# Seven half-size products instead of eight for the second feed-forward layer, in a DeltaNet kernel with a pipelined feed-forward

## The chip, the cores and the metric

The kernel runs on one core of a Trainium2 chip. The metric is the device time of one execution in microseconds (us). Each kernel is run several times beside the kernel before on the same chip; quoted are medians with the lowest and highest run. The granted clock is the share of PE's full clock rate that a trace shows as granted. Engines are named as in the profile: PE (TensorE matmuls), PEld (its weight loads), DVE (VectorE), ACT (ScalarE), POOL (GpSimd).

## The reference

Everything is fp32: a DeltaNet attention, whose state depends on every earlier token, then a feed-forward network with exact gelu.

```python
# batch, n_heads, seq, head_dim = 4, 8, 768, 48;  d_model, d_ff = 384, 2048
for t in range(S):
    kt, vt, bt = k_n[:, :, t], v[:, :, t], beta[:, :, t, None]
    y[:, :, t] = einsum('bhd,bhde->bhe', q[:, :, t], state)
    v_old = einsum('bhde,bhd->bhe', state, kt)
    state = state + bt[..., None] * einsum('bhd,bhe->bhde', kt, vt - v_old)
x = y as (3072 tokens, 384)
h = x @ w_in                          # (3072, 2048)
g = 0.5 * h * (1 + erf(h / sqrt(2)))
out = g @ w_out                       # (3072, 384)
```

## The kernel before

The sequence is cut into 12 chunks of 64 tokens. A chunk has two units (`a` = 0, 1) of 128 rows: two batches of 64 tokens each. The attention of a later chunk runs beside the feed-forward of an earlier one; a plan gives each step a time, steps are emitted in that order, DVE keeps this order exactly, and a scheduler orders PE. In this document **window w** is the stretch from the first matmul of the hidden layer (psH) of chunk w-1 to that of chunk w. Every second window, the odd ones from 3 to 9, holds an elimination: DVE inverts 32x32 triangles of two chunks row by row. Even windows hold the join, in which PE makes larger inverses from these (psJ, two levels).

```python
def products(u, part=(0, 1)):          # K K^T and K Q^T in one product of 128 columns
    ...
    nc.tensor.matmul(psG[HALF[p], r, j, cols], lhsT=u.KQt[rows, p, j, 0, :],
                     rhs=u.KQt[rows, p, j].rearrange("q x n -> q (x n)")[:, cols], ...)
    ...                                # P, the masked K Q^T: one DVE product per unit

def eliminate(j):                      # 30 rows, a chain on DVE
    nc.vector.tensor_tensor(tmp, ..., op=ALU.mult)
    nc.vector.tensor_tensor(nu[:, j + 1:, 0:j], nu[:, j + 1:, 0:j], tmp, op=ALU.add)

def back(x):                           # three transposes on DVE: XM, then Zf twice
    ...
def join(g, ts, level):                # psJ on PE: needs XM, then Zf
    ...

def fc1(c, f):                         # hidden layer, f = 0..15
    for m in range(NM):
        nc.tensor.matmul(psH, lhsT=w_in_sb[:, m, f*128:(f+1)*128], rhs=xTs[c][:, m, :], ...)
    nc.scalar.activation(gs[f], psH, ACT.Gelu)

def fc2(u, f0, f1):                    # second layer: 16 products of 384 columns per unit
    for f in range(f0, f1):
        nc.tensor.matmul(u.psO, lhsT=gs[f][:, u.a*128:(u.a+1)*128], rhs=w_out_sb[:, f, :], ...)
    if f1 == NF:
        nc.scalar.copy(o_sb, u.psO)    # then two stores
```

Of the kernel before, what the change touches and what calls it, by code (L numbers as in the profile page):

```python
# [16 lines left out]
def kernel(  # L17
# [47 lines left out]
    start = ExitStack()  # L65
    su = start.enter_context(tc.tile_pool(name="su", bufs=2))
# [4 lines left out]
    def sq(name, *shape):  # L71
        return ps.tile([128, *shape], F32, tag="sq", name=name)


    NKS, NQS, NKW = 6, 4, 10
    Kp = [cpool.tile([128, H, C], F32, name=f"Kp{i}") for i in range(NKS)]


    KQb = [cpool.tile([128, 2, NP, 2, 2, HB], F32, name=f"KQb{i}") for i in range(NQS // 2)]
    Qp = [b.rearrange("q p j x h n -> q (p j x h n)").rearrange("q (o h n) -> q o h n", o=2, h=H)[:, o]  # L80
          for b in KQb for o in range(2)]
# [9 lines left out]
    K_late = []  # L91
# [7 lines left out]
    for c in range(NC):  # L99
        for a in range(NA):  # L100
            u = tiles[c, a] = Unit()
            u.c, u.a, u.n = c, a, c * NA + a
            u.t = (c % 2) * NA + a
            u.Qp = Qp[u.n % NQS]
            u.KQb = KQb[a]
            if u.n < NKW:
                u.Kp = Kp[u.n % NKS]

    def load(c):
        if c >= NC:  # L110
            return
        for a in range(NA):
            u = tiles[c, a]
            if u.n >= NKW:
                u.Kp = K_late[(u.n - NKW) % len(K_late)]
            fetch_in(u.Kp[:, :, 0:D], k, u)
            if c < 4:
                fetch_in(u.Qp[:, :, 0:D], q, u)

    def load_blocks(c):  # L120
        for a in range(NA):
            u = tiles[c, a]
            for x, src in enumerate((k, q)):
                src = src.rearrange("b h t d -> (b h) t d")[2 * a * H:2 * (a + 1) * H]
                for h in range(2):
                    rows = slice(c * C + h * HB, c * C + (h + 1) * HB)
                    for r in range(2):
                        for e in range(2):
                            w = min(HB, D - e * HB)
                            to = slice((2 * r + e) * HB, (2 * r + e + 1) * HB)  # L130
                            nc.sync.dma_start(
                                out=u.KQb[to, :, :, x, h, 0:w].rearrange("q p j n -> q (p j) n"),
                                in_=src[r::2, rows, e * HB:e * HB + w].rearrange("n t d -> t n d"))
# [38 lines left out]
    Zf = [cpool.tile([128, NU, C], F32, name=f"Zf{i}") for i in range(2)]  # L172
    St = cpool.tile([128, NA, 2, NP, D], F32)
# [82 lines left out]
    def squares(u, n, engine=None):  # L256
        kd = u.Kp[:, :, 0:D]
        ksq = wk.tile([128, H, D], F32, tag="ksq", name="ksq")
        if engine is None:
            nc.scalar.activation(ksq, kd, ACT.Square)  # L260
        else:
            engine.tensor_tensor(ksq, kd, kd, op=ALU.mult)
        nc.vector.tensor_reduce(n, ksq, axis=AX.X, op=ALU.add)
# [33 lines left out]
    def transposed(u, part=(0, 1)):  # L297
        if 0 in part:
            u.KQt = wk.tile([128, 2, NP, 2, C], F32, tag="KQt", name="KQt", bufs=6)
        for x in part:  # L300
            psT = sq("psT", NP, 128)
            flat = (u.Kp, u.Qp)[x].rearrange("q h d -> q (h d)")
            for j in range(NP):
                nc.tensor.transpose(psT[:, j, :], flat[:, j * 128:(j + 1) * 128], ident)
            nc.scalar.copy(u.KQt[:, :, :, x, :].rearrange("q p j n -> q j p n"),  # L305
                           psT.rearrange("q j (p n) -> q j p n", p=2))

    def turned(u):
        u.KQt = wk.tile([128, 2, NP, 2, C], F32, tag="KQt", name="KQt", bufs=6)
        nc.vector.transpose(u.KQt.rearrange("q p j x n -> q (p j x n)"),  # L310
                            u.KQb.rearrange("q p j x h n -> q (p j x h n)"))

    def products(u, part=(0, 1)):
        g = u.c // 2
        cols = slice(part[0] * C, (part[-1] + 1) * C)
        psG = dn("psG").rearrange("q r (j n) -> q r j n", j=NP)
        for j in range(NP):
            for r, p in QUADS:
                rows = slice(r * C, r * C + D)
                nc.tensor.matmul(psG[HALF[p], r, j, cols], lhsT=u.KQt[rows, p, j, 0, :],  # L320
                                 rhs=u.KQt[rows, p, j].rearrange("q x n -> q (x n)")[:, cols],
                                 start=True, stop=True)
        if 0 in part:
            if u.t == 0:
                Gs[g] = wk.tile([128, NU, HB], F32, tag="G", name="G", bufs=1)
            span = slice(u.t * H, (u.t + 1) * H)
            nc.scalar.copy(heads(Gs[g][:, span]), psG[:, :, :, HB:C])
            if g > 0:
                if u.t == 0:
                    Ds[g] = wk.tile([128, NU, HB], F32, tag="diag", name="diag", bufs=1)  # L330
                nc.scalar.copy(heads(Ds[g][:, span]), psG[:, :, :, 0:HB])  # L331
                for p in range(2):
                    lower = slice(p * C + HB, (p + 1) * C)
                    nc.scalar.copy(Ds[g][lower, span], Gs[g][lower, span])
        if 1 in part:
            u.P = wk.tile([128, H, C], F32, tag="P", name="P", bufs=6)
            if u.c < 2:
                nc.scalar.copy(heads(u.P), psG[:, :, :, C:])
            else:
                nc.vector.tensor_tensor(heads(u.P), psG[:, :, :, C:], heads(mask_h), op=ALU.mult)  # L340

    def grams(us):
        for u in us:
            products(u)
# [4 lines left out]
    def diagonals(u):  # L349
# [4 lines left out]
        for j in range(NP):  # L354
            for b in range(2):
                for r, p in QUADS:
                    rows = slice(r * C, r * C + D)
                    blk = u.KQt[rows, p, j, 0, b * HB:(b + 1) * HB]
# [84 lines left out]
    def gram_steps(c):  # L443
        us = [tiles[c, a] for a in range(NA)]
        return ([(1.0, transposed, u) for u in us] if c < 4 else []) + [(2.0, grams, us)]
# [17 lines left out]
    def against_state(us):  # L463

        for u in us:
# [8 lines left out]
            for x in range(2):  # L474
                for j in range(NP):
                    for r, p in QUADS:
                        rows = slice(r * C, r * C + D)
                        to = HALF[p ^ (j % 2)] if x else HALF[p]
                        nc.tensor.matmul(u.psK[to, x, r, j, :], lhsT=u.KQt[rows, p, j, x, :],  # L479
# [90 lines left out]
    gs = {}  # L570

    def fc1(c, f):
# [4 lines left out]
        gs[f] = wk.tile([128, NA * 128], F32, tag=f"g{f}", name=f"g{f}", bufs=1)  # L577
        nc.scalar.activation(gs[f], psH, ACT.Gelu)  # L578

    def fc2(u, f0, f1):  # L580
        if f0 == 0:
            u.psO = ps.tile([128, DM], F32, tag="mlp", name="psO")
        for f in range(f0, f1):
            nc.tensor.matmul(u.psO, lhsT=gs[f][:, u.a * 128:(u.a + 1) * 128],  # L584
                             rhs=w_out_sb[:, f, :], start=(f == 0), stop=(f == NF - 1))
        if f1 == NF:
            o_sb = wk.tile([128, DM], F32, tag="o_sb", name="o_sb")
            nc.scalar.copy(o_sb, u.psO)  # L588
            for p in range(2):
                row = (2 * u.a + p) * S + u.c * C  # L590
                nc.scalar.dma_start(out=out[row:row + C, :], in_=o_sb[HALF[p]])

    def ffn_steps(c):
        steps = [(1.3, fc1, c, f) for f in range(NF)]
# [3 lines left out]
        return steps + twos  # L598
# [47 lines left out]
    for u in first:  # L646
        products(u, (0,))
    for u in first:
        transposed(u, (1,))
        products(u, (1,))  # L650
# [38 lines left out]

    def late():  # L690
        start.close()
        more = ctx.enter_context(tc.tile_pool(name="late", bufs=1))
        for i in range(4):
            K_late.append(more.tile([128, H, C], F32, name=f"Kl{i}"))
            nc.gpsimd.memset(K_late[i][:, :, D:], 0.0)
        K_late.extend(Kp)
# [6 lines left out]
    plan += [at(0.99, 1.0, [(1.0, prep, 2)]), at(1.055, 1.06, [(1.0, finish, 2)]), at(1.6, 1.61, [(1.0, finish, 3)]), at(2.75, 2.76, [(1.0, finish, 4)]), at(1.06, 1.14, gram_steps(2)),  # L703
# [3 lines left out]
             at(2.6, 2.61, [(1.0, prep, 4)]), at(2.8, 2.9, gram_steps(4))]  # L707
    plan += [at(1.62, 1.63, [(1.0, load, 4)]), at(0.995, 1.0, [(1.0, load_v, 2)])]
    plan += [at(c - 0.4, c - 0.3, v_steps(c)) for c in range(2, NC)]
    plan += [at(c - 1.0, c - 0.99, [(1.0, load_v, c)]) for c in range(3, NC)]  # L710
    plan += [at(c - 2.4, c - 2.39, [(1.0, load, c)]) for c in range(5, NC)]
    for c in range(4, NC):
        when = {4: 2.73, 5: 3.03}.get(c, c - (1.6 if c % 2 == 0 else 2.03))
        after = {4: 1.8, 5: 2.76}.get(c, c - (2.94 if c % 2 == 0 else 2.54))
        plan += [at(after, after + 0.01, [(1.0, load_blocks, c)])]
        plan += [at(when, when + 0.02, [(1.0, turned, tiles[c, a]) for a in range(NA)])]
    for w in range(3, NC):
        plan += [at(w + 0.25, w + 0.95, state_steps(w))]
        if w + 2 >= NC:
            continue  # L720
        if w % 2:
            plan += [at(w - 0.16, w - 0.15, [(1.0, prep, w + 2)]), at(w, w + 0.01, [(1.0, finish, w + 2)]),
                     at(w + 0.06, w + 0.2, gram_steps(w + 2)),
                     at(w + 0.2, w + 0.95, eliminate_steps(w // 2 + 1)),
                     at(w + 1.02, w + 1.2, join_steps(w // 2 + 1))]
        else:
            plan += [at(w + 0.35, w + 0.36, [(1.0, prep, w + 2)]), at(w + 0.5, w + 0.51, [(1.0, finish, w + 2)]),
                     at(w + 0.45, w + 0.9, gram_steps(w + 2))]
# [32 lines left out]
```

## Time and profile before

| | before |
|---|---|
| median | 717.74 us (717.25 to 717.81, 3 runs) |
| profiled span | 717.4 us |
| PE, DVE busy | 93%, 55% |
| odd windows 3, 5, 7, 9 | 50.0 us each |
| even windows 4, 6, 8, 10 | 54.9, 54.8, 54.8, 52.7 us |
| windows 11, 12 | 46.8, 45.8 us |

The busy shares and slices, and the windows, are shown in the prediction below. Beside them the page gives the chain of work that ended last, followed back from the end of the program, first by engine and then by line:

```profile
PE 74%; DVE 3%; ACT 2%; issue 0%
PE psO L584 32%; PE psH L575 28%; PE psJ L426 3%; PE psK L479 3%; PE psG L320 2%; PE psU L505 2%; PE psY L523 1%; DVE Nu L386 1%; DVE tmp L384 1%; ACT Zf L441 1%; PE psY L532 1%; PE psX L561 1%; DVE XM L395 0%; ACT g L578 0%; DVE Nu L377 0%
```

Nearly the whole chain is PE, and the two feed-forward layers (psO and psH) are 60% of the span. So the second layer looks like the place to save.

### The profile page before, as it was taken

Reading aid. Unit: us, or ns where it says so; the run is one execution under the profiler, and the core shown is the slowest. Engines: PE = TensorE matmul, PEld = TensorE weight load, DVE = VectorE, ACT = ScalarE, POOL = GpSimd, SP = SyncE. Lnnn points to the kernel's source line nnn. Section 1 sums busy time; section 2 is a strip of 40 time slices with the busy share of each in tenths; the row PEclk is TensorE's granted clock in tenths of the full one; section 3 lists DMA queues with packets and bytes.
Section 4 is the critical chain, followed back from the end, with each engine's and each line's share of the span. In section 5 each row is a group of like instructions: output and inputs, shape, how many; then the busy total and the mean of one; then the engine's idle time right before and its main releaser. Section 6 shows DMA issues by size and latency. Waiting matters only on the chain.

```text
span 717.4 us, 19222 instructions
## 1 busy us (share of the span) xinstructions
PE 667.7 (93%) x8404; PEld 496.9 (69%) x8404; DVE 392.5 (55%) x871; ACT 225.3 (31%) x570; POOL 84.7 (12%) x91
## 2 busy tenths in 40 slices
PE   6549797798999999999999999999999999999997
PEld 5447563485678678678678677687687687686774
DVE  6989999999347963337942437933547911211000
ACT  3326453431434124342132333133243133132210
POOL 5051000311301020011020110020211000000000
PEclk9999899997999999999999999999999999999999
DMA  9906735430244201441102441002201000000000
GB/s 139 227 2 145 207 89 155 92 67 1 43 59 63 52 14 26 71 58 28 35 14 32 70 56 24 13 13 40 42 12 24 13 13 2 22 3 12 12 1 22
DMA packets 137252, 36.06 MB, mean 50 GB/s; under 512 B 130064, under 2 KB 133136, under 8 KB 137168
## 3 DMA queue, kind: packets, MB, share of 16 engines
q1 hardware_dynamic: 131120, 29.52, 21.6%
q10 hardware_dynamic: 5952, 5.12, 3.0%
q8 instruction: 66, 1.08, 0.6%
q0 software_dynamic: 96, 0.20, 0.1%
q14 instruction: 18, 0.15, 0.1%
HBM read 30.08 MB, written 4.72 MB: 49 GB/s over the span
## 4 chain that ended last, share of the span: by engine, by line
PE 74%; DVE 3%; ACT 2%; issue 0%
PE psO L584 32%; PE psH L575 28%; PE psJ L426 3%; PE psK L479 3%; PE psG L320 2%; PE psU L505 2%; PE psY L523 1%; DVE Nu L386 1%; DVE tmp L384 1%; ACT Zf L441 1%; PE psY L532 1%; PE psX L561 1%; DVE XM L395 0%; ACT g L578 0%; DVE Nu L377 0%
## 5 line engine op out<-in xcount | busy, mean ns | idle before, releaser
L584 PE MATMUL psO<-w_out_sb,g 128*128 128x384 f32 x768 | 266.0, 496 | 7.5 <-DVE w_out_sb L226 7.3
L575 PE MATMUL psH<-xT,w_in_sb 128*128 128x256 f32 x1152 | 264.5, 386 | 4.1 <-DVE w_in_sb L226 2.5
L575 PEld LDWEIGHTS psH<-xT,w_in_sb 128*128 128x128 f32 x1152 | 216.7, 191 | 41.1 <-ACT g L578 4.5
L584 PEld LDWEIGHTS psO<-w_out_sb,g 128*128 128x128 f32 x768 | 142.6, 192 | 100.7 <-DVE w_out_sb L226 13.9
L578 ACT ACTIVATE g<-psH 128x256 f32<-128x256 f32 x192 | 73.7, 384 | 152.5 <-PE psH L575 151.8
L485 DVE TENSOR_TENSOR W<-psK,V 128x384 f32<-128x384 f32 x22 | 12.2, 553 | 99.6 <-PE psK L479 74.6
L384 DVE TENSOR_TENSOR tmp<-Nu 128x30 f32<-128x30 f32 (+9 forms) x180 | 62.6, 348 | 6.0
L386 DVE TENSOR_TENSOR Nu<-Nu,tmp 128x30 f32<-128x30 f32 (+9 forms) x180 | 61.5, 342 | 6.2
L340 DVE TENSOR_TENSOR P<-psG,mask 128x512 f32<-128x512 f32 x20 | 13.6, 690 | 79.4 <-ACT diag L331 79.3
L274 POOL TENSOR_TENSOR n<-n,half 128x16 f32<-128x16 f32 x10 | 29.5, 2947 | 93.8 <-DMA Zf<-in_moe_w_out_dram 60.6
L546 DVE TENSOR_TENSOR x<-psY,y 64x192 f32<-64x192 f32 x88 | 31.1, 353 | 17.2 <-PE psY L523 16.3
L511 ACT COPY U<-psU 64x192 f32<-64x192 f32 x92 | 28.8, 313 | 33.4 <-PE psU L505 32.1
L294 POOL TENSOR_TENSOR V<-V,n 128x384 f32<-128x384 f32 x20 | 16.8, 844 | 185.6 <-DMA V<-in_v_dram 114.4
L588 ACT COPY o_sb<-psO 128x384 f32<-128x384 f32 x24 | 11.5, 480 | 81.0 <-PE psO L584 79.7
L562 ACT COPY xT<-psX 128x384 f32<-128x384 f32 x24 | 11.3, 478 | 81.2 <-PE psX L561 81.2
L320 PE MATMUL psG<-KQt 48*64 48x128 f32 (+1 forms) x896 | 28.7, 285 | 4.1 <-ACT KQt L305 2.7
L320 PEld LDWEIGHTS psG<-KQt 48*64 48x64 f32 x896 | 24.9, 157 | 10.3 <-issue 4.3
L426 PE MATMUL psJ<-XM,G 32*32 32x32 f32 x768 | 15.6, 203 | 14.9 <-DVE XM L395 14.9
L217 ACT ACTIVATE w_e<-w_e,lim 128x384 uint32<-128x384 uint32 (+2 forms) x31 | 19.3, 625 | 28.8 <-DVE w_e L215 28.7
L408 POOL MEMSET Zf<- 32x512 f32 x23 | 12.2, 529 | 130.1 <-DVE Zf L399 99.1
L426 PEld LDWEIGHTS psJ<-XM,G 32*32 32x32 f32 x768 | 14.8, 119 | 17.3 <-POOL W L469 11.6
L479 PEld LDWEIGHTS psK<-St,KQt 48*64 48x64 f32 x1408 | 22.1, 137 | 6.1 <-issue 4.0
(97 smaller groups left out, 535.5 us busy)
## 6 DMA issues: line engine op xcount, KB each, us to landing
V<-in_v_dram SPq DMA_DIRECT2D x48, 96.0 KB, 3.0
w_out_sb<-in_moe_w_in_dram SPq DMA_DIRECT2D x9, 512.0 KB, 5.5
out_dram<-o_sb ACTq DMA_DIRECT2D x48, 96.0 KB, 2.2
Zf<-in_moe_w_out_dram SPq DMA_DIRECT2D x8, 384.0 KB, 4.2
w_raw<-in_moe_w_out_dram SPq DMA_DIRECT2D x8, 384.0 KB, 3.8
Kp<-in_k_dram SPq DMA_DIRECT2D x28, 96.0 KB, 4.0
KQb<-in_k_dram SPq DMA_DIRECT2D x64, 32.0 KB, 2.2
KQb<-in_q_dram SPq DMA_DIRECT2D x64, 32.0 KB, 2.2
```

The costliest lines, as they stand in the source:

```text
L217: nc.scalar.activation(e, e, ACT.Relu, bias=lim[:, 0:1], scale=float(2 ** 23))
L274: nc.gpsimd.tensor_tensor(flat, flat, half, op=ALU.pow)
L320: nc.tensor.matmul(psG[HALF[p], r, j, cols], lhsT=u.KQt[rows, p, j, 0, :], rhs=u.KQt[rows, p, j].rearrange("q x n -> q (x n)")[:, cols], s ...
L384: nc.vector.tensor_tensor(tmp, nu[:, j + 1:, j:j + 1].to_broadcast([128, n, j]), nu[:, j:j + 1, 0:j].to_broadcast([128, n, j]), op=ALU.mult)
L386: nc.vector.tensor_tensor(nu[:, j + 1:, 0:j], nu[:, j + 1:, 0:j], tmp, op=ALU.add)
L426: nc.tensor.matmul(psJ[to, i // (2 * H), i % (2 * H), :], lhsT=(xm if level else off)[rows, u, :], rhs=zf[rows, u, HB:C] if level else xm[ ...
L479: nc.tensor.matmul(u.psK[to, x, r, j, :], lhsT=u.KQt[rows, p, j, x, :], rhs=St[rows, u.a, p, j, :], start=True, stop=True)
L511: copy(pairs(u.U[HALF[p]], s), u.psU[HALF[p ^ s], p])
L546: nc.vector.tensor_tensor(dst, src, pairs(u.y[HALF[p ^ s]], s), op=ALU.add)
L575: nc.tensor.matmul(psH, lhsT=w_in_sb[:, m, f * 128:(f + 1) * 128], rhs=xTs[c][:, m, :], start=(m == 0), stop=(m == NM - 1))
L578: nc.scalar.activation(gs[f], psH, ACT.Gelu)
L584: nc.tensor.matmul(u.psO, lhsT=gs[f][:, u.a * 128:(u.a + 1) * 128], rhs=w_out_sb[:, f, :], start=(f == 0), stop=(f == NF - 1))
```

## The change

The intent is to save an eighth of the second layer on PE. Unit a of a chunk gives the rows of a 2x2 block matrix, the halves of the 2048 hidden values its columns, `a11 a12 / a21 a22`; w_out is cut likewise into B11, B12, B21, B22. Winograd's form of Strassen's scheme makes the product from seven half products p1 to p7, each of 8 matmuls of 192 columns (two instructions each), with sums before and after:

```diff
+    def sums_of_w():                  # once, on POOL: T1 = B12-B11, T2 = B22-T1, T4 = B21-T2
+        for n, a, b in ((1, B12, B11), (2, B22, 1), (4, B21, 2)):
+            T[n] = more[0].tile([128, FH, DH], F32, name=f"T{n}")
+            nc.gpsimd.tensor_tensor(T[n], a, b if n == 1 else T[b], op=ALU.subtract)
+    def last_sum_of_w():              # T3 = B22-B12
+    ...
+    def mix(c, n, h):                 # DVE, 128x512 each, in two halves
+        if n == 1:                    # S = a21+a22;  a21 <- a11-a21
+            nc.vector.tensor_tensor(W2["S"][:, fs], a21, a22, op=ALU.add)
+            nc.vector.tensor_tensor(a21, a11, a21, op=ALU.subtract)
+        elif n == 2:                  # a11 <- S-a11, once p1 has read a11
+            nc.vector.tensor_tensor(a11, W2["S"][:, fs], a11, op=ALU.subtract)
+        else:                         # a12 <- a12-a11
+            nc.vector.tensor_tensor(a12, a12, a11, op=ALU.subtract)
+    def two(c, n):                    # X: p1+p2, and p4;  Z: p5+p3;  Y: p6+p7
+    ...
+    def read2(c, n):                  # u2 = Y+p1 after p6; u3 = Y+p1 after p7; four outputs
+    ...
     def ffn_steps(c):
-        steps = [(1.3, fc1, c, f) for f in range(NF)]
+        ones = [(1.3, fc1, c, f) for f in range(NF)]
+        if c > 1:
+            k = NF - FH // 2
+            return ones[:k] + [(0.1, mix, c, 1, 0)] + ones[k:] + [
+                (0.1, mix, c, 1, 1), (2.6, two, c, 1), (2.6, two, c, 5), (0.1, mix, c, 2, 0),
+                (0.1, mix, c, 2, 1), (2.6, two, c, 6), (2.6, two, c, 2), (0.1, read2, c, 2),
+                (0.1, mix, c, 3, 0), (0.1, mix, c, 3, 1), (2.6, two, c, 7), (2.6, two, c, 4),
+                (0.1, read2, c, 7), (2.6, two, c, 3), (0.1, read2, c, 4), (0.1, read2, c, 3)]
```

To fit the memory for this, the joint transposed tile of K and Q is split. K products (for chunk w+2) and query products P (for chunk w) become two runs of 64-column products; the transposed K and Q are made apart, and P and Q only one chunk ahead:

```diff
-    def turned(u):                    # K and Q in one transpose
+    def turned_k(u):
+    def turned_q(u):
...
-                     at(w + 0.06, w + 0.2, gram_steps(w + 2)),
+        if w + 2 < NC:
+            steps += [(1.0, grams, [tiles[w + 2, a] for a in range(NA)])]
+        plan += [at(w + 0.06, w + 0.2, steps + [(1.0, queries, us)])]
```

The code above is cut; pools, loads and buffers change with it.

## The prediction

> **What bounds the kernel now.** I read the page's busy times and 40 slices first, to find the stage that matters.
>
> ```profile
> PE 667.7 (93%) x8404; PEld 496.9 (69%) x8404; DVE 392.5 (55%) x871; ACT 225.3 (31%) x570; POOL 84.7 (12%) x91
> ...
> PE   6549797798999999999999999999999999999997
> ...
> DVE  6989999999347963337942437933547911211000
> ```
>
> From the tenth slice (about 200 us) PE never rests, while DVE swings between full and a third. PE issue is the bound there; before that it is mostly DVE (decoding weights). Next I cut the steady stage at the first psH matmul of each chunk, found in PE's timeline, and asked for the busy time in those windows (us; then PE, PEld, DVE, ACT, POOL busy with counts).
>
> ```profile
> 257.70:312.60 54.90, 54.84 (x807) 41.34 (x806) 19.57 (x37) 18.68 (x48) 9.53 (x8) 1.00 0.27 42
> 312.60:362.60 50.00, 50.00 (x552) 37.25 (x551) 36.17 (x83) 14.56 (x40) 3.57 (x3) 1.00 0.21 36
> 362.60:417.40 54.80, 54.74 (x807) 41.23 (x806) 19.07 (x37) 18.71 (x48) 9.53 (x8) 1.00 0.27 43
> ...
> 671.60:717.40 45.80, 41.56 (x161) 30.21 (x159) 0.00 (x0) 7.59 (x19) 0.00 (x0) 0.99 0.06 13
> ```
>
> Windows alternate: 50.0 us (call it odd; DVE inverts a 32x32 triangle row by row, 36 us busy) and 54.8 us (even; DVE light). Four pairs follow, then two windows without elimination. The third view is DVE's timeline of the odd window at 312.6.
>
> ```profile
> 319.74 0.69 DVE L340 TENSOR_TENSOR P<-psG,mask 128x512 f32<-128x512 f32 x1 [10.26 <-ACT diag L331]
> ...
> 331.72 0.56 DVE L485 TENSOR_TENSOR W<-psK,V 128x384 f32<-128x384 f32 x1 [3.49 <-PE psK L479]
> 332.31 0.56 DVE L486 TENSOR_TENSOR W<-W,gm 128x384 f32<-128x384 f32 x1
> ...
> 336.85 0.90 DVE L384 TENSOR_TENSOR tmp<-Nu 128x210 f32<-128x210 f32 x1
> ...
> 347.50 0.38 DVE L384 TENSOR_TENSOR tmp<-Nu 128x210 f32<-128x210 f32 x1
> ...
> 357.96 2.07 DVE L395 STREAM_TRANSPOSE XM<-Nu 128x1024 f32<-128x1024 f32 x1
> 359.91 3.69 DVE L399 STREAM_TRANSPOSE Zf<-Nu 128x1024 f32<-128x1024 f32 x2
> 367.52 2.85 DVE L437 TENSOR_TENSOR XM<-psJ,gm 32x512 f32<-32x512 f32 x4 [3.92 <-PE psJ L426]
> ```
>
> From 331.7 to 363.6 DVE has no gap. Its chain ends 51.0 us into a window of 50.0, and only because PE wants nothing from it before psJ at 365 does nobody wait. This hidden tie decides the case.
>
> **What the Trainium skill says.** "TensorE: Matmul & The Clock Gate", Back-to-back issue gap, gives N/2.4+2.5 ns warm for a pass. Here an fp32 matmul is two instructions; 64 of 384 columns span 20.80 us in the last chunk's timeline, and (20.80-0.486)/63 = 322.5 ns, which is 384/1.2+2.5: two passes each. Groups of 256 and 128 columns give 215 and 109: the same line. "SBUF — State Buffer", section "two separate sides": the port pair shared by VectorE and GpSimd is an exclusive lock for a VectorE operation with two SBUF inputs. The trace agrees: the 210-element product took 0.90 us while POOL scaled V (336.69 to 337.52), and 0.38 us in another row. "VectorE: DVE Perf Modes", Mode 2×_2P, says fp32 tensor_tensor stays at one element per cycle; 128x384 takes 558 ns and 64x192 353, so 1.07 ns per element plus 148, and 128x512 is 692 here. The first page, "What's actually happening", says PE falls to half clock after some 3.4 us idle; the trace agrees:
>
> ```profile
> 171.55 3.63 PE L426 MATMUL psJ<-XM,G 32*32 32x32 f32 x128 [3.53 <-DVE XM L395]
> 175.10 5.48 PE L584 MATMUL psO<-w_out_sb,g 128*128 128x384 f32 x8
> 180.51 2.21 PE L426 MATMUL psJ<-Zf,XM 32*32 32x32 f32 x128
> ```
>
> The same 128 instructions cost 3.63 us after 3.5 us of idling and 2.21 warm.
>
> **The change part by part.**
>
> (1) PE, second layer, ten chunks. Before: 64 instructions x 322.5 = 20.64 us. After: 7 x 8 matmuls x 2 = 112 instructions of 192 columns x 162.5 (192/1.2+2.5) = 18.20. Saved: 2.44 us per chunk. I choose the streaming rate though one weight load is listed at 190 ns: in the transposes loads last 141 ns at a pitch of 109, so successive loads overlap.
>
> (2) PE, P and Q products split. 64 instructions of 128 columns cost 1.98 us; now 64+64 of 64 columns. psU, also 64 columns of weights, does 64 in 1.15 us, so 2.3 us: +0.33 per chunk. Net saving 2.1 us per chunk, 21 in all if PE alone set the time.
>
> (3) DVE, every Strassen chunk: eight mixes of 128x512 (0.69 us) and five reads of 128x192 (0.35): about 7.2 us busy. P's two masks merge; transposes become four of 512 instead of two of 1024, and in odd windows all four land in the window (+2.6). Odd: 36.2+7.2+2.6 = 46 us busy against a PE need of 47.5 (50.0-2.1, less p3's 2.6 that moves out, plus psJ's 2.2 that moves in). That leaves no room for DVE's own waits.
>
> (4) Those waits, by the order in which the changed kernel compiles (DVE and PE are both in order). In an odd window, from its first psH: 9 psH, K products, 6 psH, P products, so the mask starts at 9.1 (7.1 before). Mask, flip and five rows as timed before: 16.7. W waits for psK: 17.9 to 20.1. Row 6 and, after the twelfth gelu, the first mix: 22.3. Eight rows: 30.0; mix: 31.3; PE wanted the second half of S at 30.4. Seven rows and mixes of A11: 37.4, 38.1, 39.7; PE wanted p6 at about 34, a stall of 4 us. Five rows 43.0, state and x 46.9, two rows and u2 48.3 (p7 waits for u2), mixes 49.7, last row and XM 52.1 (psJ waits), Zf 55.8, u3 and an output add 56.5, K transposes 57.8, X read 58.2. The next chunk's first psH needs that psum buffer, so the window lasts 58.2 us: 10.6 of stall. Even window: 54.8+2.6-2.2-2.1 = 53.1. Pair: 111.3 instead of 104.8, +6.5; four pairs +26.
>
> (5) PE idles over 3.4 us at p6 and at the next chunk's start. The second cold restart falls where PE is the bound; by the psJ rows I allow 1.5 us per pair: +6.
>
> (6) Sums of w_out on POOL, 128x1536 three times, run right after the first XM (its wait list has nothing later), during elimination 1. At 1.91 us per 1024 elements (XM) each takes 2.9 us and locks DVE out: up to 8.6 us on a chain for which psJ already waits 3.53 us. I count +7.
>
> (7) Last two windows, PE-bound: -4.2. The end keeps its shape: one DVE add replaces an ACT copy of 0.48 us.
>
> Sum: 717.7+26+6+7-4.2 = 752.5. I take 749, a little less because steps 5 and 6 are upper readings.
>
> **Rivals.** A: PE stays the bound and mixes hide; 717.7-21 = 697, the intent. For it: PE is full in every steady slice and DVE averages 55%; S has a whole p1 to be made in. Against it: the gapless 32 us of DVE. B: weight loads of 190 ns bind; then 112 x 190 = 21.3 us, PE gains nothing, and with DVE's waits about 770. C: the queue order hurts less than I chain it (odd windows 53 us): -4 instead of +6.5+1.5 per pair with the POOL sums half hidden, around 712. D: more DMA, since K is read in rows twice: bandwidth is at 0.2 to 0.3 share in these windows, so I give it nothing.
>
> **Range and chances.** Each us of error in the odd chain counts four times; 3 us either way gives 12, the POOL sums and cold clock another 5 or so. Range 731 to 765. Slower by over 2% starts at 732.1: 0.82; within 2%: 0.12; faster: 0.06.
>
> **What would show it.** Right: windows by first psH near 58 and 53 us; PE idle before p6, psJ and the first psH released by DVE, none in the last two windows; the 192-column pitch at 162 to 163 ns; DVE rows of elimination 1 stretched to 3 us beside POOL; the first psJ of the second chunk's window late by 7 to 9 us more. Wrong: odd windows near 47.5 us (DVE hid it, the answer is A), or a pitch of 190 (B), or transposes waiting for DMA (D).

## The result and the profile after

The changed kernel took 748.96 us (median of 4 runs, 747.81 to 752.09) against 717.77 (717.25 to 720.72). The ratio is 1.0433, with a 95% interval of 1.039 to 1.0475: slower. The output is correct. The page of the profiled run (span 745.8 us):

```profile
PE 664.3 (89%) x9524; PEld 573.5 (77%) x9524; DVE 468.0 (63%) x1007; ACT 215.7 (29%) x530; POOL 99.5 (13%) x93
...
PE   5549796794999799999799999799999799999997
...
DVE  5989989999436982457982448983448961413321
...
PE 54%; DVE 38%; issue 4%; DMA 1%; ACT 1%; POOL 0%; SPq 0%; ACTq 0%; POOLq 0%; DVEq 0%
```

PE's row now has a 7 in every steady pair of windows, just where DVE shows 8 or 9, and DVE's share of the chain that ended last rose from 3 to 38%. The same windows as in the prediction (length, then PE, PEld, DVE, ACT, POOL busy with counts, granted clock, DMA share, GB/s), here 5, 6, 11 and 12:

```profile
328.90:384.10 55.20, 50.95 (x776) 45.96 (x774) 44.62 (x100) 13.52 (x36) 3.91 (x4) 0.94 0.22 37
384.10:438.90 54.80, 53.33 (x806) 48.47 (x807) 24.11 (x48) 17.79 (x44) 9.29 (x8) 1.00 0.32 53
656.40:702.50 46.10, 45.91 (x536) 41.85 (x535) 14.56 (x28) 11.31 (x32) 0.00 (x0) 1.00 0.04 10
702.50:745.80 43.30, 39.11 (x210) 36.34 (x208) 7.59 (x14) 6.76 (x18) 0.00 (x0) 0.99 0.07 15
```

The odd window 5 grew from 50.0 to 55.2 us with PE idle for 4.3 of it. The even window kept its length. Window 12, where PE alone counts, shrank by 2.5, which is the intended gain. All windows, in us, with the experiments to come:

| kernel | 1 | 2 | 3 | 4 | 5 | 6 | 7 | 8 | 9 | 10 | 11 | 12 |
|---|---|---|---|---|---|---|---|---|---|---|---|---|
| before | 84.2 | 63.8 | 50.0 | 54.9 | 50.0 | 54.8 | 50.0 | 54.8 | 50.0 | 52.7 | 46.8 | 45.8 |
| after | 87.6 | 69.3 | 56.0 | 55.5 | 55.2 | 54.9 | 55.4 | 53.9 | 55.1 | 53.0 | 46.1 | 43.3 |
| split_only | 87.8 | 56.1 | 51.2 | 58.2 | 50.3 | 54.9 | 50.3 | 54.8 | 50.3 | 57.0 | 48.1 | 45.8 |
| sums_late | 84.1 | 60.4 | 55.5 | 55.4 | 54.0 | 56.2 | 54.0 | 56.6 | 54.0 | 54.7 | 46.1 | 43.4 |
| mix_early | 85.0 | 68.2 | 56.2 | 53.8 | 55.3 | 57.0 | 55.3 | 53.9 | 55.3 | 53.0 | 46.1 | 43.3 |
| zf_late | 86.4 | 68.0 | 54.7 | 55.1 | 52.5 | 56.1 | 52.7 | 55.1 | 53.4 | 54.3 | 46.1 | 43.3 |
| dve_pad | 83.5 | 70.0 | 58.2 | 55.5 | 57.2 | 56.4 | 57.2 | 55.3 | 57.3 | 54.4 | 46.1 | 43.3 |
| even_only | 84.2 | 60.4 | 51.2 | 56.3 | 50.3 | 56.1 | 50.3 | 54.6 | 50.3 | 52.5 | 46.1 | 43.3 |
| even_shift | 83.9 | 60.3 | 51.2 | 53.5 | 50.3 | 53.4 | 50.3 | 53.4 | 50.3 | 52.5 | 46.1 | 43.3 |
| even_q_u2 | 86.1 | 60.4 | 51.2 | 53.0 | 50.3 | 53.0 | 50.3 | 53.0 | 50.3 | 51.6 | 45.6 | 43.3 |

From before to after the profiled span grew by 28.4: the four odd windows +22.0, the four even ones 0.0, window 2 +5.5, the last two -3.2, window 1 and the start some +4. Window 1 can't be put down to the change: over the variants, which share nearly all of its code, it varies from 83.3 to 87.8 (the kernel before was profiled once, with 84.2). What makes it vary was not looked into.

PE's waits (line waited for; us in total, times, longest) name the odd windows' cause:

```profile
PE psJ L451 <- DVE XM L420: 21.8, 2, 11.3
PE psY L647 <- DVE G L659: 16.1, 4, 4.0
...
PE psH L609 <- DVE u L692: 2.8, 4, 1.4
```

G at L659 is the mix of a11, for which p6 waits 4.0 us in each of the four odd windows. The wait for XM was there before (14.9 us in all), but 6.9 shorter. DVE's timeline of window 5 (start, duration, instruction; the window starts at 328.9):

```profile
337.94 1.22 DVE L369 TENSOR_TENSOR P<-psG,mask 128x1024 f32<-128x1024 f32 x1 [6.13 <-PE psG L334]
...
365.98 0.68 DVE L659 TENSOR_TENSOR G<-S,G 128x512 f32<-128x512 f32 x1
...
378.04 2.12 DVE L420 STREAM_TRANSPOSE XM<-Nu 128x1024 f32<-128x1024 f32 x1
380.04 3.71 DVE L424 STREAM_TRANSPOSE Zf<-Nu 128x1024 f32<-128x1024 f32 x2
383.60 0.33 DVE L692 TENSOR_TENSOR u<-psY,p 128x192 f32<-128x192 f32 x1
```

After the mask DVE works through without a pause worth naming, except 1.6 us before W. The elimination, the mixes, the reads of the attention, the transposes and u3 (L692) queue one behind the other. PE in the same window:

```profile
366.71 5.49 PE L647 MATMUL psY<-T,G 128*128 128x192 f32 x16 [4.03 <-DVE G L659]
...
384.08 0.67 PE L609 MATMUL psH<-xT,w_in_sb 128*128 128x256 f32 x2 [0.22 <-DVE u L692]
```

p6 waits 4.03 us, then takes 5.49 instead of 2.76 (p1 in this window); the trace has a granted clock of 0.5 for 6.8 us from just before it. The next chunk's psH starts when u3 is done. PE comes there only 0.2 us before DVE (1.35, 0.67 and 0.60 in the other odd windows): the two engines finish the window nearly together.

### The profile page after: what moved, and what is told of

It is laid out like the page before. It is cut to its first block, busy times and chain, and to the rows that moved or that the text cites. A ratio compares the mean times of both kernels' runs of the same rounds, so it can differ in the third digit from the quotient of the medians.

```text
span 745.8 us, 21696 instructions
## 1 busy us (share of the span) xinstructions
PE 664.3 (89%) x9524; PEld 573.5 (77%) x9524; DVE 468.0 (63%) x1007; ACT 215.7 (29%) x530; POOL 99.5 (13%) x93
## 4 chain that ended last, share of the span: by engine, by line
PE 54%; DVE 38%; issue 4%; DMA 1%; ACT 1%; POOL 0%; SPq 0%; ACTq 0%; POOLq 0%; DVEq 0%
PE psH L609 25%; DVE tmp L409 8%; DVE Nu L411 8%; PE psZ L647 6%; PE psX L647 5%; PE psY L647 4%; DVE x L576 3%; PE psO L622 3%; PE psG L334 3%; PE psK L509 2%; PE psJ L451 2%; DVE Zf L424 2%; DVE XM L420 2%; DVE w_e L230 1%; PE psU L535 1%
## 5 line engine op out<-in xcount | busy, mean ns | idle before, releaser
L611 ACT ACTIVATE G<-psH 128x256 f32<-128x256 f32 x192 | 73.6, 383 | 191.6 <-PE psH L609 150.0
L622 PE MATMUL psO<-w_out_sb,G 128*128 128x384 f32 x128 | 51.0, 544 | 9.6 <-DVE w_out_sb L231 9.6
L647 PE MATMUL psX<-w_out_sb,G 128*128 128x192 f32 x320 | 56.2, 329 | 0.0
L647 PEld LDWEIGHTS psX<-w_out_sb,G 128*128 128x128 f32 x320 | 52.3, 190 | 1.0
L647 PE MATMUL psY<-T,G 128*128 128x192 f32 x160 | 37.3, 401 | 16.1 <-DVE G L659 16.1
L622 PEld LDWEIGHTS psO<-w_out_sb,G 128*128 128x128 f32 x128 | 25.3, 209 | 29.7 <-DVE w_out_sb L231 15.3
L369 DVE TENSOR_TENSOR P<-psG,mask 128x1024 f32<-128x1024 f32 x10 | 12.2, 1224 | 56.9 <-PE psG L334 56.8
L647 PEld LDWEIGHTS psY<-T,G 128*128 128x128 f32 x160 | 35.0, 243 | 16.5 <-DVE G L659 16.5
L656 DVE TENSOR_TENSOR S<-G 128x512 f32<-128x512 f32 x20 | 13.8, 690 | 37.2 <-ACT G L611 37.2
L567 DVE TENSOR_TENSOR St<-St,psY 128x384 f32<-128x384 f32 x22 | 12.1, 552 | 34.9 <-PE psY L562 34.7
```

What stands on the lines that cost most here:

```text
L611: nc.scalar.activation(G[:, f, :], psH, ACT.Gelu)
L622: nc.tensor.matmul(u.psO, lhsT=G[:, f, u.a * 128:(u.a + 1) * 128], rhs=w_out_sb[:, f, :], start=(f == 0), stop=(f == NF - 1))
L647: nc.tensor.matmul(ps_, lhsT=lhs[:, f, :], rhs=rhs[:, f, :], start=first and f == 0, stop=f == FH - 1, skip_group_check=not first)
```

## The experiments

Twelve kernels were run. The short names are the labels.

### split_only: the change without Strassen

```diff
-        if c > 1:                     # in ffn_steps
+        if c > NC:
...
-    plan += [at(0.995, 1.0, [(1.0, load_v, 2)]), at(2.96, 3.0, [(1.0, last_sum_of_w)]),
-             at(2.5, 2.51, [(1.0, sums_of_w)])]
+    plan += [at(0.995, 1.0, [(1.0, load_v, 2)])]
```

> The changed kernel without Strassen in any chunk and without the sums of w_out; P and Q still split and late, K read twice. Theory: 64+64 products of 64 columns cost 2.3 us where 64 of 128 cost 1.98, so +0.33 us in ten chunks; the stretch before the second chunk, 3.4 us longer in the changed kernel, comes from this part too if it returns here. So 721 to 725 us. Rival: the loss sits in this part (double K loads, late P); then 735 us or more. PE should show no idle time in the odd windows (50 us as before).

Measured: 725.26 us (723.69 to 728.2) against 716.87, ratio 1.0117 [1.008, 1.0153], 0.3 us over the expected range. The odd windows 5, 7 and 9 are 50.3 us, within 0.3 of before, without a wait for DVE; window 3 is 51.2. So the split and the early transposes don't make the odd windows long; the seven products do. Two windows, 4 and 10, are 58.2 and 57.0, where 55 and 53 were to be expected; it returns below.

### sums_late: POOL's sums of w_out after the first elimination

POOL is given the order of the plan, so that its sums run at 2.5, not as soon as their inputs are there.

```diff
-    with tc.manual_schedule(engines={mybir.EngineType.DVE}):
+    with tc.manual_schedule(engines={mybir.EngineType.DVE, mybir.EngineType.Pool}):
```

> The changed kernel with POOL's order fixed by hand, so that the three sums of w_out run after elimination 1 instead of beside it. Theory (the sums lock the vector engine out: three operations there took 4.44, 3.30 and 3.32 us instead of 1.2, 0.2 and 0.2, and the first psJ waited 10.5 us and ran cold): 9.4 us of lock and about 1.4 us of cold clock go, so 738 us. Rival (the sums are hidden and elimination is late for another reason): 748 us.

Measured: 734.09 us (732.17 to 736.89), ratio 1.0238 [1.0198, 1.0278]. Window 2 went from 69.3 to 60.4. In the kernel after, the sums ran from 147.67 to 159.05 us and the elimination beside them stood still. POOL's timeline of that stretch:

```profile
147.67 3.44 POOL L633 TENSOR_TENSOR T<-w_out_sb 128x1536 f32<-128x1536 f32 x1
151.19 7.86 POOL L633 TENSOR_TENSOR T<-w_out_sb,T 128x1536 f32<-128x1536 f32 x2
```

DVE's timeline beside it:

```profile
147.76 4.44 DVE L402 TENSOR_TENSOR Nu<-Nu,XM 128x1024 f32<-128x1024 f32 x1 [0.68 <-POOL XM L396]
152.23 3.30 DVE L409 TENSOR_TENSOR tmp<-Nu 128x30 f32<-128x30 f32 x1
```

The row product of 128x30 takes 0.21 us in the other eliminations and 3.30 here; the first, of 128x1024, 1.22 and 4.44. With a third (3.32 instead of 0.22) that makes 9.4 us in which DVE held still for POOL, and moving the sums gave back 8.9 in window 2. What it did to PE is seen in the kernel after, in the first psJ of window 2, which had waited 3.53 us before:

```profile
182.63 3.62 PE L451 MATMUL psJ<-XM,G 32*32 32x32 f32 x128 [10.54 <-DVE XM L420]
```

This part is shown. The time is 4 us below the 738 expected: window 1, with the start, was 4.1 shorter in this profile than in that of the kernel after. Fixing POOL's order also moved the later windows (the odd ones 1.1 us shorter on average, the even ones 1.4 longer), which no step of this argument uses.

### mix_early: the mixes of a11 ahead in DVE's order

If p6's wait for its mix is what makes the odd window long, the mix should come earlier.

```diff
-                (0.1, mix, c, 1, 1), (2.6, two, c, 1), (2.6, two, c, 5), (0.1, mix, c, 2, 0),
-                (0.1, mix, c, 2, 1), (2.6, two, c, 6), ...
+                (0.1, mix, c, 1, 1), (0.02, two, c, 1), (0.1, mix, c, 2, 0), (0.1, mix, c, 2, 1),
+                (5.18, two, c, 5), (2.6, two, c, 6), ...
```

> The changed kernel with the two mixes of A11 right behind the mixes of S in the vector engine's order, ahead of some seven rows of elimination; same work. p6 should no longer wait. Theory one (the vector engine's whole chain through the odd window, up to u3 after the Zf transposes, sets its length; the p6 wait is only where PE meets it first): the odd windows stay within 1 us of 55.2, the time stays within 3 us of 749. Theory two (the p6 wait of 4.0 us and the 2.7 us of half clock after it are the loss): odd windows 48.5 us, the time near 722 us.

Measured: 744.02 us (743.3 to 744.4), ratio 1.0372 [1.0347, 1.0398]. The odd windows are 56.2, 55.3, 55.3, 55.3: unchanged, as theory one has it. The time is 2 us below its range of 746 to 752; in the profile windows 1 and 2 with the start are 4.3 us shorter, and the other windows together 0.9 longer. The wait for the mix is gone from the list of PE's waits, and another has its place:

```profile
PE psX L591 <- DVE x L576: 20.0, 6, 4.6
```

PE now waits as long for the attention's output x, which DVE makes later in its queue. So p6's stall was a symptom. The time is set by the length of DVE's queue, not by which of its products PE waits for first.

### mix_small: mixes and S on 8 of 128 columns (wrong)

```diff
-        a11, a12, a21, a22 = (A[a][k][:, fs] for ...)
+        a11, a12, a21, a22 = (A[a][k][:, fs, 0:8] for ...)
```

> Wrong results on purpose: each mix covers 8 of 128 columns, so it takes about 0.18 us instead of 0.69; the order of everything is kept. Theory (the vector engine's added work sets the odd windows): eight mixes save 4.1 us, p6 waits 1.5 us instead of 4.0 and the clock stays up; odd windows 51 us, 728 us in all. Rival (position in the queue or PE itself sets it): odd windows stay near 55 us, 745 to 749 us.

Measured: 742.54 us (741.42 to 746.06), ratio 1.0369 [1.033, 1.0408]; the result is wrong, as intended. DVE's queue did end 4.0 us earlier (Zf done 50.9 us into window 5 instead of 54.9), but the scheduler, which knows the sizes, ordered PE anew: p3 came before the next psH, with waits of 1.4 us for an output sum and 1.1 for u2, and p6 still waited 2.8. Odd windows: 57.9, 54.2, 54.1, 55.7. The miss does not speak against the queue as the cause, nor for it: two things changed. An experiment on such a kernel has to hold PE's order.

### zf_late and both: shorten what comes last in the queue

Zf isn't needed until psJ's second level, which is in the next window. In zf_late its two transposes (3.7 us) come behind the reads at the end of the odd window; both adds the edit of mix_early.

```diff
-                     at(w + 0.2, w + 0.95, eliminate_steps(w // 2 + 1)),
+                     at(w + 0.2, w + 0.2 + 0.75 * 26.3 / 30.1, eliminate_steps(w // 2 + 1)[:-2]),
+                     at(w + 0.9972, w + 0.9978, zf_steps(w // 2 + 1)),
```

> The changed kernel with the two Zf transposes (3.7 us) of each odd window moved behind the reads of the chunk's products, so that u3 comes 3.7 us earlier. Theory (two ends meet: the vector engine's chain releases the next psH only 0.2 us after PE, held up 4.0 us at p6 and 2.7 us by half clock, gets there): moving one of the two alone gives little, 746 to 750 us, odd windows near 55. Rival (the chain's tail alone sets the window): odd windows 51.5 us, 734 us.

> The mixes of A11 early and the Zf transposes late together. With the mixes early alone, PE waited 4.6 us for x and 1.5 us for u3 per odd window. Theory (the vector engine is full from W to u3, so each reorder moves the wait to the next operand it makes): the 1.5 us go, the wait for x stays; odd windows 53.5 us, 736 to 741 us. Rival (both ends of a pair are now open): odd windows 48.5 us, about 720 us.

Measured: zf_late 739.06 us (738.31 to 739.78), ratio 1.0289 [1.0272, 1.0306] with before at 718.11; both 741.34 (739.44 to 746.5), ratio 1.0336 [1.0296, 1.0376]. PE's timeline in window 5 of zf_late:

```profile
362.46 4.26 PE L650 MATMUL psY<-T,G 128*128 128x192 f32 x16 [4.04 <-DVE G L662]
...
377.10 0.70 PE L612 MATMUL psH<-xT,w_in_sb 128*128 128x256 f32 x2
```

The last psH wait is gone, and odd windows 5, 7 and 9 are 52.5 to 53.4, so 1.7 to 2.7 shorter, and not 3.7. Some 1.1 us of that is half of psJ that slipped into the next window. What remains is PE's own path: it still waits 4 us for the mix, and runs p6 slowly after. In the kernel after, the two paths ended 0.2 to 1.35 us apart, so taking from one soon shows the other. In both, the wait moved to x again (20.0 us in six waits), and its odd windows are 53.0 to 53.7. Its time is 0.3 us over its range; that of zf_late is 7 us under its own, so the tail of the queue was worth more than I had thought.

### dve_pad: more on DVE's queue

Four idle products of 128x384 follow the mixes of a11 in each odd window.

```diff
+    def pad(c):
+        if c in (2, 4, 6, 8):
+            for i in range(4):
+                nc.vector.tensor_tensor(W2["D"], w_in_sb[:, 0, 0:384], w_in_sb[:, 1, 0:384], op=ALU.mult)
-                (0.1, mix, c, 2, 1), (2.6, two, c, 6), ...
+                (0.1, mix, c, 2, 1), (0.0, pad, c), (2.6, two, c, 6), ...
```

> The changed kernel with four idle products of 128x384 on the vector engine in each odd window, behind the mixes of A11 and ahead of the state; about 2.0 us per window, results right. Theory (the vector engine sets the odd windows): each window grows by about its 2 us, 8 us in all, 757 us. Rival (PE sets them): no change, 749 us.

Measured: 759.69 us (756.08 to 760.43), ratio 1.057 [1.0542, 1.0598]. The four products take 2.33 us as a row:

```profile
365.97 2.33 DVE L666 TENSOR_TENSOR D<-w_in_sb 128x384 f32<-128x384 f32 x4
```

The odd windows are 58.2, 57.2, 57.2 and 57.3, which is 1.8 to 2.2 longer each. Every us added to DVE's queue in an odd window is nearly a us of the window. This shows directly that DVE's queue sets the odd windows of the changed kernel; that a us taken off the queue doesn't give a whole us back, zf_late showed. The even windows also grew, by 4.4 us in all, where nothing was added; the time is 2.7 us over the 757 expected.

### even_only: Strassen only where DVE is light

If so, the seven products belong only into the windows without an elimination.

```diff
-        if c > 1:
+        if c > 1 and (c % 2 or c > 9):
```

(T3 gets its own tile, POOL the planned order as in sums_late, and scratch tiles share room.)

> Strassen only in the chunks whose window has no elimination (4th, 6th, 8th, 10th, 11th and 12th), the sums of w_out after elimination 1, B12 kept and the fourth sum in its own tile; some scratch tiles merged for the room. Theory: six times 2.4 us less on PE, 3.3 us more for the split P and Q, 1 to 4 us more before the second chunk; odd windows 50.3 us with no PE wait, even windows 52.8; 706 to 713 us. Rival (mixes stall PE in light windows too): even windows above 54 us, 718 us or more.

Measured: 716.74 us (716.01 to 717.41), ratio 0.9982 [0.9967, 0.9997]. The odd windows are 50.3 without waits, as expected (window 3: 51.2). But the even ones were to be 52.8 and are 56.3, 56.1, 54.6, 52.5: the expected gain was missing there. PE in window 4:

```profile
265.89 2.21 PE L451 MATMUL psJ<-Zf,XM 32*32 32x32 f32 x128
268.03 0.79 PE L334 MATMUL psG<-Qt,Kt 48*64 48x64 f32 x35
269.84 0.69 PE L334 MATMUL psG<-Qt,Kt 48*64 48x64 f32 x29 [1.02 <-issue]
270.46 9.69 PE L609 MATMUL psH<-xT,w_in_sb 128*128 128x256 f32 x36
```

In the midst of the query products PE pauses for 1.02 us, and the profile shows nothing that it waited for ("issue"). The psH matmuls after it come 427 ns apart, six times, before they return to 216. In the kernel before, psJ's second level is followed by psH; here the split and the new order put the 64 query products right behind it, which makes a run of 192 small matmuls and as many weight loads. The same pause, of 1.38 us from matmul to matmul, was in window 4 of split_only. Its other long window, 10, was something else: psH waited 1.20 us for a gelu, and then ran slowly too.

### even_q, even_q_u2 and split_q: take the query products out of the dense run

```diff
-        plan += [at(w + 0.06, w + 0.2, steps + [(1.0, queries, us)])]
+        plan += [at(w + 0.06, w + 0.2, steps + [(1.0, queries, us)][:w % 2])]
+        if w % 2 == 0:
+            plan += [at(w + 0.46, w + 0.47, [(1.0, queries, us)])]
```

even_q_u2 also puts u2, for which p7 waited 0.7 us in each even window, right behind p6:

```diff
-                (2.6, two, c, 6), (2.6, two, c, 2), (0.1, read2, c, 2),
+                (2.6, two, c, 6), (0.1, read2, c, 2), (2.6, two, c, 2),
```

> even_only (Strassen in even windows only) with one thing moved: in even windows the queries' products P no longer follow the level-2 psJ products directly but come at 46% of the window, with hidden-layer products between. Theory (dense run: some 190 small matmuls with as many weight loads in a row are followed by a pause of 1.0 to 1.2 us called issue, then about 3 us of hidden-layer products at half clock): the pauses before the first psG of windows 4, 6, 8 and 10 go, the even windows shorten by 2 to 3 us each, and the kernel takes 707 to 711 us. Rival (the pause comes from something else in the even windows, the second level of psJ alone or the clock's own limits): windows 4, 6, 8, 10 stay at 54.6 to 56.3 us and the kernel at 715 to 717.

> even_q with the read of p6 into u2 placed right after p6 in the order, ahead of p2, so that DVE makes it before p7 needs it. Theory: p7's wait of 0.7 to 0.8 us for u2 goes in every even window, 3 to 4 us less than even_q, 704 to 708 us, and faster than the kernel before by 1.4 to 1.9%. Rival (the wait only moves to another product that needs a free psum buffer): the same time as even_q within 0.2%.

> split_only (no Strassen; P and Q split and transposed early) with the queries' products moved in even windows as in even_q. Theory of the dense run: windows 4 and 10, which were 58.2 and 57.0 us in split_only, go back to about 55.2 and 53.0, the kernel to 718 to 722 us, at most 0.6% over the kernel before. Rival: unchanged at 724 to 726 us.

Measured, against 717.27 (716.68 to 719.8): even_q 711.98 us (711.34 to 714.39), ratio 0.9923 [0.9904, 0.9941]; even_q_u2 707.98 (707.68 to 709.89), ratio 0.9868 [0.9849, 0.9887]; split_q 722.7 (722.02 to 725.55), ratio 1.0077 [1.0057, 1.0096]. In even_q the pauses are gone and windows 4, 6 and 8 are 53.9; in even_q_u2 the waits for u2 are gone too, and they are 53.0, close to the 52.8 that the arithmetic gave. Window 4 of split_q fell from 58.2 to 55.6. The three moved as expected; even_q and split_q are 1.0 and 0.7 us over their ranges (in split_q the wait in window 10 stayed, and the moved products made windows 6 and 8 some 0.6 longer).

**even_q_u2 is faster than both kernels**: 1.3% under the kernel before (the interval excludes 1), and 5.4% under the changed one by the ratio of these ratios (0.9868 / 1.0433); the two were not run side by side.

### even_shift: is it the run, or where it is cut?

That a long run of small matmuls makes PE pause says not yet why. The page of even_only has a row for a DMA queue that carries instructions (packets, MB, share of 16 engines' time):

```profile
q8 instruction: 73, 1.20, 0.7%
```

1.20 MB in 73 packets is 16 KiB each, as the packet records say. PE ran 9332 matmuls, 9332 weight loads and 94 instructions for semaphores and the like; 18758 / 73 is 257. Before, 16894 / 66 is 256.0. So a packet carries about 256 of PE's instructions. The Trainium skill, "Runtime: NRT & Kernel Launch", Instruction fetch mechanics, has this: blocks of 16 KiB or 256 instructions, fetched while earlier ones run. It calls the fetch hidden, since instructions are dispatched more slowly than they come. In psJ that is not so: 256 instructions take 2.21 us. I counted PE's instructions (matmuls, loads and semaphore instructions) up to each pause of more than 0.7 us, from start to start, inside a run of small matmuls for which the profile names no engine, from 204 us on, in all profiled runs:

```
kernel      pauses  place of the first instruction      us from the landing of the last
                    after the pause, modulo 256         instruction packet to that instruction
after       1       193                                 1.38
split_only  1       193                                 1.40
sums_late   2       193, 193                            1.26, 1.34
mix_early   2       193, 193                            1.47, 1.33
zf_late     1       193                                 1.23
both        1       193                                 1.57
dve_pad     2       193, 193                            1.30, 1.41
even_only   3       193, 192, 193                       1.24, 1.44, 1.19
before, mix_small, even_q, even_q_u2, split_q: none
```

The place is always the same one of 256, and the end of the pause always 1.2 to 1.6 us behind a landing. That is what a boundary of blocks looks like (the one 192 is 193 too when the count is by start times). mix_small is listed with none only because its pause, at the same place (193) and 1.42 us after a landing, lies just behind such a run, in psH. The landings of all blocks say the same: in the 14 profiles there are 758 instructions at place 193 from 204 us on, and none started less than 1.18 us after the packet of its block's number had landed. The pauses lie at this lower edge. even_only repeats itself every 3072 instructions, or 12 whole blocks, so all its three pauses lie alike. If this is right, it is enough to move the boundaries. In even_shift the K products of chunk 0 are made twice, in the first stage, where PE has time: 128 more instructions. The order of every engine's instructions is otherwise the same.

```diff
-                for r, p in QUADS:
+                for r, p in [t for t in QUADS for _ in range(2 if u.c == 0 and not x else 1)]:
```

> even_only with one thing added: the K products of chunk 0 are made twice, 64 more small matmuls with their weight loads (128 more instructions on PE's queue) in the first stage, where PE is half idle; every engine's order is otherwise the same. In even_only the three pauses of 1.0 to 1.3 us in windows 4, 6 and 8 fell at PE instruction 7105, 10176 and 13249, which is 193 or 192 modulo 256 each time, and each ended 1.2 to 1.4 us after a 16 KiB packet of the instruction queue (256 instructions) had landed. Theory (PE runs out of fetched instructions when a whole block of 256 falls inside the run of 384 small ones): 128 more instructions ahead move the block boundaries to the middle of that run, no whole block lies in it, the pauses and the half clock after them go, windows 4, 6 and 8 take about 53.9 us as in even_q instead of 56.3, 56.1 and 54.6, and the kernel takes 710 to 713 us although it does more work. Rival (the dense run itself, or the clock, makes the pause): the pauses stay, 716 to 718 us.

Measured: 711.61 us (710.18 to 713.4) against 717.47, ratio 0.9922 [0.9901, 0.9943]. Against even_only's 0.9982 the kernel that does more work is 0.6% faster. The same place in window 4:

```profile
265.78 2.21 PE L451 MATMUL psJ<-Zf,XM 32*32 32x32 f32 x128
267.92 1.16 PE L334 MATMUL psG<-Qt,Kt 48*64 48x64 f32 x64
269.01 8.04 PE L609 MATMUL psH<-xT,w_in_sb 128*128 128x256 f32 x36
```

The run of 384 instructions is as dense as before, with no pause in it, and the 36 psH instructions behind it take 8.04 us instead of 9.69. Windows 4, 6 and 8 lost 2.8, 2.7 and 1.2 us. The rival, that the dense run itself makes the pause, has fallen: PE had waited for its own instructions. It happens where a block of 256 lies within such a run, all or nearly all of it (248 or more of the 256 instructions before each of the 13 pauses were of small matmuls, and they were passed in 2.1 to 3.4 us); in even_shift the run is cut in its middle.

## Why the prediction was right

The measured median, 748.96, is the predicted 749. Not every term was right; by the numbers of the prediction's steps:

1. **Second layer.** Right: the 192-column instructions come every 163 ns where nothing else is in the way, and window 12 lost 2.5 us (2.44 predicted). Weight loads of 190 ns don't bind, so rival B is out.
2. **Split products.** Right: 64 products of 64 columns take 1.16 us.
3. **DVE's load.** Right within 1.4: 44.6 us busy in window 5, 46 predicted.
4. **The chain in odd windows.** Right up to its last leg, and the heart of it confirmed by dve_pad. Into the window, predicted and measured: mask 9.1 and 9.1; stall at p6 4 and 4.03; XM done 52.1 and 51.3; Zf done 55.8 and 54.9; u3 56.1 and 55.1. The step that failed is the last: "K transposes 57.8, X read 58.2. The next chunk's first psH needs that psum buffer, so the window lasts 58.2 us". The trace shows that psH waited for u3 only, and started at 55.2. This term was 3.0 us too large in window 5, and 2.7 on average over the four odd windows, 11 in all: they gained 5.5 on average, not 8.2. A smaller piece failed too: psJ did not wait for XM, since PE, held up and slowed at p6, reached psJ only 52.8 us into the window.
5. **Cold clock.** The first restart was right, the charged one mostly did not come. p6 lost 1.8 to 2.7 us to half clock in each odd window, but beside DVE's longer queue. The second restart, at the next chunk's start, was charged with 1.5 us per pair, 6 in all. It needed an idle time of over 3.4 us there; the waits were 1.35, 0.22, 0.67 and 0.60. Only after the longest did p3 run slowly, 4.33 us instead of 2.76, in window 4: 1.6 us in all. The even windows are 54.3 on average, for 53.1 + 1.5 predicted; the rest of the surplus is p7's wait for u2 (0.7 in each even window, 2.7 in all) and a pause for instructions in window 6 (1.0), and neither was in the prediction. That the even windows cost nearly what was reckoned is luck.
6. **POOL's sums.** Right in kind, and the locking too low: 9.4 us on DVE, where up to 8.6 was reckoned and 7 counted. The duration of a sum was scaled from XM, 1.91 us per 1024, to 2.9; it took 3.44. One of XM's operands is broadcast, and the sum's are not; whether that is the reason was not tested. The Trainium skill, "GPSIMD Engine Reference", Elementwise — side-by-side cycle accounting, has 4497 ns for 2048 elements of a two-input sum; an estimate from it is 3.37 for 1536. The first psJ of window 2 was late by 7.0 us more (10.54 us of wait instead of 3.53), as step 6 wanted. Window 2 grew by only 5.5, because it was shorter without the sums, 60.4 in sums_late, than before, 63.8; the split is the likely reason, not isolated here.
7. **The last two windows.** -3.2, not -4.2: the query products of chunk 11 moved into window 11 (1.16 us).

The sum was 752.5, 34.8 over before; measured in the profiles are 28.4. The pairs of windows were 10 us too large (32 predicted, 22.0 measured), POOL's sums with the end 0.5 too large (2.8 predicted, 2.3 measured), and 4 us came from window 1, which no step had and which varies between profiles. That 749 was hit to a tenth is luck in part; that it is slower, by what and where, was read from the profile. The taking of 749 instead of 752.5 "because steps 5 and 6 are upper readings" was right in sum for another reason, the last leg of step 4.

Rival C's sum does not come out as written: with odd windows of 53 us a pair is 106.1, so 1.3 above 104.8 and not 4 below, and the kernel would take about 722, not 712. Of the rivals, A (PE stays the bound) holds in windows 11 and 12, and in the even windows once their small waits are out, as even_q_u2 showed. D is out: from window 3 on, DVE's transposes waited 1.0 us in all for a DMA, 0.4 at most, where DVE has time (in window 5 it then waits 6.13 us for PE). What stays open is why an odd window with the seven products could not be brought under 52.5 us in zf_late and both; the waits that remained there are named, but no run took them all away. It also stays open what exactly delays an instruction by 1.2 us behind its packet's landing.

## What to carry to other kernels

An engine that is full in every slice hides a second one that is a tenth of a window behind; before giving work from the first to the second, follow the second's queue through the window from end to end, not its average share. Do it where the second engine is idle: the same change, in the even and the last two windows only, with POOL's sums later, the query products out of the dense run and u2 earlier, gained 1.3% where everywhere it lost 4.3% (even_only, with the place and POOL's order alone, brought 0.2%). When PE pauses for "issue" in a run of small matmuls, count its instructions, semaphore instructions included, modulo 256 before looking for a wait.

## What the Trainium skill lacked or had wrong

- "Runtime: NRT & Kernel Launch", Instruction fetch mechanics: it calls the fetch hidden behind the pace of dispatch. Here PE passes 256 instructions of small matmuls and loads in 2.21 us, and 13 pauses of 0.8 to 1.6 us at block boundaries were seen; each ended 1.2 to 1.6 us after the block's packet had landed. Moving the boundaries by 128 instructions removed three of them, and 0.6% of the time. The page names a stall for fetching at taken branches only.
- "TensorE: Matmul & The Clock Gate", What's actually happening: half clock after an idle window of some 3.4 us. In even_only, after a pause of 1.0 us behind 163 small matmuls, the psH instructions in window 4 still came 427 ns apart, six times, instead of 216 (granted clock 0.70 to 0.74 over the 6 us from the pause on). It was so in window 6 too, after 0.94 us, but not in window 8: there, after 1.09 us, they came at 216 and the clock stayed at 1.0. Without the pause, in even_shift, they came at 216. What decides between the two was not tested.
- The same page, Back-to-back issue gap: it gives no pace for fp32 (the four passes of a full fp32 product stand in "FP8 and Floating Point Precision", TensorE Precision Notes; two instructions of two passes each fit them). Here it is N/1.2+2.5 ns per instruction, two instructions per matmul, each with its weight load: 163 ns for 192 columns, with weight loads listed at 190 ns each, which did not bind.
- "SBUF — State Buffer", two separate sides, has the exclusive lock, and the trace agrees; it has no example of what it does to a chain of DVE products: three of one elimination took 4.44, 3.30 and 3.32 us instead of 1.22, 0.21 and 0.22.
